# Weighted sums of an attention block moved from the scores' PSUM banks to the mix's banks, and inverse sums turned in row halves

## The chip, the cores and the metric

The kernel runs on one core of a Trainium2 chip. The metric is the device time of one execution in microseconds (us). Four compute engines work side by side, each through its own instructions in order: PE (matrix products, with its weight loads as a row of their own, PEld), DVE (vector), ACT (activations and copies) and POOL (elementwise work in SBUF). Transfers are issued from a fifth queue, SP. Results of PE land in PSUM, which has eight banks here, each of 512 fp32 values per partition.

## The reference, cut to what matters

```
# attention: q, k, v are (8 batches, 8 heads, 576, 64)
scores = q @ k.T / sqrt(64)
scores = where(scores >= 32nd largest of its row, scores, -1e9)
attn = exp(scores - max);  attn = attn / (sum(attn) + 1e-9)
x = (attn @ v), heads side by side          # (8, 576, 512)
# channel mix on x
x_prev = x moved down by one row
xk = mu_k*x + (1-mu_k)*x_prev;  xr = mu_r*x + (1-mu_r)*x_prev
k = max(xk @ w_k, 0);  v = k*k @ w_v        # 512 -> 1024 -> 512
r = sigmoid(xr @ w_r)
out = r * v
```

## The kernel before

The attention is cut into 288 tiles: one tile is 128 query rows against all 576 keys, as scores in 2 x 288 columns. Tiles form units of four (`U.w` = 4: two heads, two blocks of 128 rows), two or one; a unit shares one reciprocal of its row sums, one set of weighted sums and one write into `xT`, the transposed attention output. There are 112 units. A software pipeline runs over slots. In slot n it takes tile n in by `score` (PE) and `keep` (ACT copies the scores to SBUF), looks for candidates of tile n-1 (DVE), ranks tile n-2 (DVE), counts tile n-3 (ACT `count`, POOL `below`), exponentiates and masks tile n-4 (ACT `exp`, DVE `mask`), and turns tile n-5 (PE `turn_tile` and an ACT copy `et`). When the tile of n-6 is the last of its unit, the slot turns the unit's inverse sums (`inv`, which calls `turn_inverse`, followed by an ACT copy `ri`) and computes its weighted sums (`weigh`, PE); one slot later ACT copies these to SBUF (`sums`, which calls `take_sums`) and POOL multiplies them by the inverse sums (`place`).

Into the same slots the channel mix is fitted. It runs over 18 chunks of 256 rows of `xT`, each with 8 pieces of gates (`pz`), 16 of hidden values (`ph`) and 16 of output values (`pv`), 720 pieces in all. A piece is three PE products of 512 columns, or six of 256 columns. A gate group is 4 pieces, a hidden group 4, a value group 8. The products accumulate in a bank of the pool `psM`, which has two banks used in turn; a group's bank is emptied one slot after its last piece by ACT (`relu`, tanh) or DVE (`stt` at the step `first`). In the first 20 slots, before the mix can start, weight blocks are split into two parts through the same banks.

The order is set by hand: the table `ORDER` says in which order the steps of a slot are written, and so in which order they stand on each engine. How many pieces of the mix a slot gets is a planner's decision (`Lanes`, `work`): each slot adds 3.90 (`TENSOR`) to PE's budget, each step takes its own cost off (`L.use`), a piece costs 0.71, and pieces are written while the budget allows, at most 4 a slot. In the last 36 slots a piece costs 0.56. The planner's numbers are fixed in the code and are no measurements.

PSUM: the scores have two banks (`psS`, the tile `ps`), the exponentials two (`psE`), the turned tiles and the turned inverse sums two (`psT`), the mix two (`psM`). The weighted sums lie in columns 288 to 415 of the scores' banks:

```
g.ps = scored[:, :, :HS]                                        # HS = 288
g.sums = scored[:, :, HS:HS + 128], scored[:, 0, HS + 128:HS + 192]
```

Of the kernel before, what the change touches and what calls it, by code (L numbers as in the profile page):

```python
# [43 lines left out]
ORDER = """count below exp wpool high wmul norm evac best0 c0 drop0 c1 best1 c2 drop1 first score turn inv loads keep sums sign c3 best2 c4 bounds eighth norm2 et late act c5 early thr c6 mask place mix weigh wpe dve pool weights""".split()  # L44
# [3 lines left out]
def topk_attention_channel_mix(ctx: ExitStack, tc: tile.TileContext, q, k, v, mu_k, mu_r, w_k, w_v, w_r, out):  # L48
# [28 lines left out]
    def open_pools(stack, g, sfx):  # L77
# [17 lines left out]
        g.psM = p("psM", 2, space=PSUM)  # L95
# [24 lines left out]
    def weight_block(g, L, n, block, hi, lo, half):  # L120
# [8 lines left out]
        def remains(*more):  # L129
            W.lo = g.psM.tile([128, 512], F32, name="wlo", tag="pm")  # L130
            nc.tensor.matmul(W.lo, lhsT=ident, rhs=valf, start=True, stop=False)
            for i, x in enumerate(more):
                nc.tensor.matmul(W.lo, lhsT=x[0], rhs=x[1], start=False, stop=i == len(more) - 1)

        def fine():
            g.ready.append(nc.scalar.activation(lo, W.lo, AF.Copy, scale=scale))

# [17 lines left out]
        def shift():  # L155
            bits = g.psM.tile([128, 512], U32, name="wbits", tag="pm")
            nc.vector.tensor_scalar(bits, mag, 3, 0x3FFFFFFF, op0=OP.logical_shift_left, op1=OP.bitwise_and)
            nc.vector.scalar_tensor_tensor(val, high, 0xC0000000, bits, op0=OP.bitwise_and, op1=OP.bitwise_or)
            nc.vector.tensor_scalar(exp, val, 0xFF800000, None, op0=OP.bitwise_and)

# [141 lines left out]
    def turn_inverse(g, U, L):  # L302
        rb = U.rb.rearrange("p h d -> p (h d)")
        pr = g.pt[:, :, 384:]
        n = (U.w + 1) // 2
        for u in range(n):
            nc.tensor.transpose(pr[:, u], rb[:, u * 128:(u + 1) * 128], ident)  # L307

        def out_():
            U.ri = g.two.tile([128, 256], F32, name="ri")  # L310
            if U.w > 1:
                nc.scalar.activation(U.ri[:, :n * 128].rearrange("p (u q) -> p u q", u=n), pr[:, :n], AF.Copy)
            else:
                for j in range(2):
                    h = slice(j * 64, (j + 1) * 64)
                    nc.scalar.activation(U.ri[h, :64], pr[h, 0, h], AF.Copy)
# [18 lines left out]
    def take_sums(g, U):  # L335
# [4 lines left out]
        else:  # L340
            nc.scalar.activation(U.sum[:, :64], U.pa, AF.Copy)

# [49 lines left out]
    def hidden(g, f, part, xh, xl, hh, hl, n, X, L):  # L392
        if part == 0:
            X.ph = g.psM.tile([128, 2, CH], F32, name="ph", tag="pm")
# [8 lines left out]
        def relu():  # L403
            X.r = g.two.tile([128, 2, CH], F32, name="r")
            nc.scalar.activation(X.r[:, :, :n], ph[:, :, :n], AF.Relu)
        out_ = L.at(1, "evac", relu, "act", 0.46)
# [4 lines left out]
    def gate(g, t, m, h, xh, xl, G, L):  # L411
        if h == 0:
            G.pz = g.psM.tile([128, DM], F32, name="pz", tag="pm")
# [5 lines left out]
        def first():  # L419
            G.e = g.four.tile([128, DM], F32, name="eb")  # L420
            nc.scalar.activation(G.e[:m], pz[:m], AF.Tanh, scale=0.5)
        G.done = L.at(1, "evac", first, "act", 0.48)

    def value(g, t, m, hh, hl, f, G, row, L):
        if f == 0:
            G.pv = g.psM.tile([128, DM], F32, name="pv", tag="pm")
# [547 lines left out]
```

## Time and profile before

| | |
|---|---|
| median of 3 runs | 1203.48 us (1203.01 to 1204.04) |
| the profiled execution, its own time | 1202.92 us |
| span of its instructions | 1201.1 us |
| PE busy | 1115.5 us (93%) |
| DVE busy | 1078.9 us (90%) |
| POOL busy | 1025.5 us (85%) |
| ACT busy | 996.3 us (83%) |
| DMA | 78.79 MB, 24% of 16 engines' time |

Read it as three stretches: up to about 158 us the weights are prepared beside the first tiles; from 158 to 1117 us attention and mix run in the same slots; after the last score (1116.56 us) the pipeline empties and the last chunks of the mix remain. The span starts 1.8 us inside the execution's own time.

### The profile page before, as it was taken

How to read it: one execution, taken by the hardware profiler on the slowest of the kernel's cores; microseconds unless marked ns; L12 is line 12 of the kernel's file. 1: busy time of each engine (PE TensorE's matmuls, PEld its weight loads, DVE VectorE, ACT ScalarE, POOL GpSimd, SP SyncE). 2: the span in 40 equal slices, each digit the busy share in tenths (PEclk: the TensorE clock that was granted, in tenths of full speed). 3: DMA queues.
4: the chain of work that ended last, by engine and by line, in shares of the span. 5: the costliest groups of instructions: out<-in, count | busy, mean ns of one | idle time of the engine just before them, and what ended most of it. 6: DMA issues, size and time to landing. Idle time of an engine off the chain costs nothing.

```text
span 1201.1 us, 33093 instructions
## 1 busy us (share of the span) xinstructions
PE 1115.5 (93%) x10625; PEld 864.1 (72%) x10625; DVE 1078.9 (90%) x6287; ACT 996.3 (83%) x2121; POOL 1025.5 (85%) x1099
## 2 busy tenths in 40 slices
PE   4777899899999999999999999999999999999987
PEld 2443577676868787878787877787878777877876
DVE  4989999999999999999999999999999999999600
ACT  3777799898988899989898989998989899978621
POOL 5999987888889898989898888898989798988863
PEclk8788699899999999999999999999999999999998
DMA  5343124122322133212221124112321133111000
GB/s 171 99 135 98 30 49 107 47 54 60 87 71 55 49 89 76 58 47 58 67 58 47 43 77 101 50 43 67 100 73 44 48 86 87 46 39 39 29 10 29
DMA packets 161366, 78.79 MB, mean 66 GB/s; under 512 B 125344, under 2 KB 154016, under 8 KB 161184
## 3 DMA queue, kind: packets, MB, share of 16 engines
q1 hardware_dynamic: 161184, 76.59, 24.0%
q8 instruction: 87, 1.43, 0.5%
q14 instruction: 95, 0.78, 0.2%
HBM read 67.11 MB, written 9.44 MB: 64 GB/s over the span
## 4 chain that ended last, share of the span: by engine, by line
PE 50%; DVE 19%; ACT 14%; POOL 13%; issue 2%; SPq 1%; DMA 1%; DVEq 0%; ACTq 0%; POOLq 0%
PE ps L333 10%; PE ps L208 7%; DVE cand L241 4%; ACT sc L217 4%; PE pv L388 4%; DVE E L271 4%; PE ph L388 4%; PE pt L283 3%; PE pv L390 3%; PE pv L389 3%; DVE top L836 3%; POOL sg L260 3%; PE ph L389 3%; PE ph L390 3%; PE pz L388 2%; ACT sg L257 2%
## 5 line engine op out<-in xcount | busy, mean ns | idle before, releaser
L241 DVE MAX8 cand<-sc 128x8 f32<-128x82 f32 (+1 forms) x2016 | 468.0, 232 | 3.2 <-ACT sc L217 2.7
L260 POOL TENSOR_TENSOR sg<-sc,sg 128x576 f32<-128x576 f32 x288 | 410.9, 1428 | 38.3 <-ACT sg L257 36.7
L217 ACT ACTIVATE sc<-ps 128x576 f32<-128x576 f32 x288 | 187.9, 652 | 92.3 <-PE ps L208 80.6
L257 ACT ACTIVATE sg<-sc,seen 128x576 f32<-128x576 f32 x288 | 225.8, 784 | 26.0 <-DVE top L836 19.7
L271 DVE SCALAR_TENSOR_TENSOR E<-sc,seen,se 128x576 f32<-128x576 f32 x288 | 233.0, 809 | 0.4
L268 ACT ACTIVATE se<-sc,seen 128x576 f32<-128x576 f32 x288 | 215.8, 749 | 17.0 <-DVE E L271 16.2
L836 DVE MAX8 top<-sg 128x8 f32<-128x576 f32 x288 | 216.5, 752 | 3.3 <-POOL sg L260 2.9
L208 PE MATMUL ps<-K,qs 64*128 64x288 f32 x1024 | 202.4, 472 | 14.5 <-ACT sc L217 6.4
L286 ACT ACTIVATE et<-pt 128x640 f32<-128x640 f32 x288 | 204.6, 710 | 6.2 <-PE pt L307 3.0
L333 PE MATMUL ps<-et,v_in 128*64 128x128 f32 (+1 forms) x2560 | 165.3, 273 | 21.4 <-ACT sc L217 18.6
L283 PEld LDWEIGHTS pt<-ident,E 64*128 64x128 f32 x2880 | 134.0, 140 | 66.7 <-ACT sg L257 16.1
L244 DVE MAX8 top<-cand 128x8 f32<-128x56 f32 x864 | 177.4, 205 | 0.1
L388 PE MATMUL ph<-xh,wk 128*128 128x256 f32 x576 | 172.0, 299 | 0.0
L333 PEld LDWEIGHTS ps<-et,v_in 128*64 128x64 f32 x2560 | 134.5, 141 | 51.3 <-ACT sc L217 37.3
L389 PE MATMUL ph<-xl,wk 128*128 128x256 f32 x576 | 163.1, 283 | 0.0
L390 PE MATMUL ph<-xh,wk 128*128 128x256 f32 x576 | 162.8, 283 | 0.0
L283 PE MATMUL pt<-ident,E 64*128 64x64 f32 x2880 | 141.3, 226 | 5.7 <-DVE E L271 3.3
L208 PEld LDWEIGHTS ps<-K,qs 64*128 64x128 f32 x1024 | 80.6, 192 | 75.0 <-issue 29.6
L388 PE MATMUL pv<-wv,hh 128*128 128x512 f32 x288 | 122.0, 424 | 0.0
L390 PE MATMUL pv<-wv,hl 128*128 128x512 f32 x288 | 114.2, 397 | 7.2 <-POOL hl L409 7.2
L384 POOL TENSOR_TENSOR xl<-xm,xh 128x512 fp32r<-128x512 f32 x72 | 91.2, 1287 | 34.6 <-ACT xh L383 34.5
L247 DVE MATCH_REPLACE8 cand<-top,cand 128x56 f32<-128x56 f32 x576 | 115.6, 201 | 0.0
(92 smaller groups left out, 2359.0 us busy)
## 6 DMA issues: line engine op xcount, KB each, us to landing
v_in<-in_v SPq DMA_DIRECT2D x192, 128.0 KB, 2.5
qs<-in_q SPq DMA_DIRECT2D x96, 128.0 KB, 2.8
K<-in_k SPq DMA_DIRECT2D x64, 144.0 KB, 3.0
out<-eb SPq DMA_DIRECT2D x36, 256.0 KB, 2.2
vr_in<-in_v SPq DMA_DIRECT2D x96, 32.0 KB, 2.4
hh<-in_moe_w_v SPq DMA_DIRECT2D x6, 512.0 KB, 3.6
qs<-in_q SPq DMA_DIRECT2D x32, 96.0 KB, 2.6
hh<-in_moe_w_k SPq DMA_DIRECT2D x5, 512.0 KB, 3.4
```

What stands on the lines that cost most here:

```text
L208: nc.tensor.matmul(g.ps[:, e], lhsT=P.qs[h, T.j, x:x + 128], rhs=P.K[h, T.j], start=True, stop=True)
L217: nc.scalar.activation(T.sc.rearrange("p (e k) -> p e k", e=2), T.ps, AF.Copy)
L241: nc.vector.max(T.cand[:, 8 * i:8 * i + 8], T.sc[:, CUTS[i]:CUTS[i + 1]])
L257: nc.scalar.activation(T.side, T.sc, AF.Sign, bias=T.under, scale=-BELOW, accum_out=T.cnt)
L260: nc.gpsimd.tensor_mul(T.side, T.sc, T.side)
L271: nc.vector.scalar_tensor_tensor(T.e, T.sc, T.thr, g.pe, op0=OP.is_ge, op1=OP.mult, accum_out=T.rs)
L283: nc.tensor.transpose(g.pt[:, n, c * 64:(c + 1) * 64], T.e[h, k0:k0 + 128], ident[h, h])
L333: nc.tensor.matmul(pa[hs[j]], lhsT=lhsT, rhs=ms[c][j], start=(c == 0), stop=(c == NKC))
L388: nc.tensor.matmul(ps, lhsT=sh, rhs=mh, start=first, stop=False)
L389: nc.tensor.matmul(ps, lhsT=sh, rhs=ml, start=False, stop=False)
L390: nc.tensor.matmul(ps, lhsT=sl, rhs=mh, start=False, stop=last)
L836: nc.vector.max(M.top[:, 24:32], M.side)
```

## The change

Five things change. (1) `psM` becomes one buffer for each of two tags, handed out in turn by `bank`, and flags in the builder (`g.full`) record whether a bank's contents have been written out. (2) `weigh` asks `borrow` for a bank: if the one that comes next in turn is marked empty and all weight blocks are ready, the weighted sums go there (a tile named `pa`); otherwise they go to the scores' banks as before. Borrowing does not advance the turn. (3) In `ORDER`, `sums` stands ahead of `keep`. (4) `turn_inverse` turns 64-row halves, two for each former transpose, into the two banks of `pt`, as `turn_tile` does. (5) The planner's costs of a unit fall by 0.25 (0.1 for single ones) and of a turn by 0.1.

```diff
-ORDER = """... turn inv loads keep sums sign c3 ..."""
+ORDER = """... turn inv loads sums keep sign c3 ..."""
...
-        g.psM = p("psM", 2, space=PSUM)
+        psM = p("psM", 1, space=PSUM)
+        g.turn, g.full = 0, [False, False]
+        def bank(shape, name, dtype=F32):
+            i, g.turn = g.turn, 1 - g.turn
+            g.full[i] = True
+            return psM.tile(shape, dtype, name=name, tag=f"pm{i}"), i
+        def borrow(shape):
+            i = g.turn
+            if g.full[i] or len(g.ready) < 3 * HP + NFB:
+                return None
+            g.full[i] = True
+            return psM.tile(shape, F32, name="pa", tag=f"pm{i}"), i
+        def free(i):
+            g.full[i] = False
...
         for u in range(n):
-            nc.tensor.transpose(pr[:, u], rb[:, u * 128:(u + 1) * 128], ident)
+            for i, h in enumerate(hs):
+                nc.tensor.transpose(pr[:, i, hs[u]], rb[h, u * 128:(u + 1) * 128], ident[h, h])
...
         if u == 0:
-            U.pa = g.sums[U.w == 1]
+            U.pa, U.at = g.borrow([128, 2, 128] if U.w > 1 else [128, 64]) or (g.sums[U.w == 1], None)
...
+        if U.at is not None:
+            g.free(U.at)
...
-                    L.use("pe", 0.9 * ((W.U.w + 1) // 2) + 0.7 if W.U.w > 1 else 0.7)
+                    L.use("pe", 0.9 * ((W.U.w + 1) // 2) + 0.45 if W.U.w > 1 else 0.6)
...
-                    L.use("pe", 0.2)
+                    L.use("pe", 0.1)
```

`bank` and `free` also stand where the mix and the weights take and empty their banks. Line numbers after the change are larger by up to 28.

On PE, in a slot with the sums of a four-tile unit (the 87th after the first), before:

```order
L208 MATMUL ps<-K,qs 128x288 x2
L283 MATMUL pt<-ident,E 128x64 x10
L307 MATMUL pt<-ident,rb 128x128 x2
L333 MATMUL ps<-et_5828,v_in 64x128
L333 MATMUL ps<-et_5887,v_in 64x128
...
L333 MATMUL ps<-et_6041,vr_in_78 64x128
L208 MATMUL ps<-K,qs 128x288 x2
```

and in the same slot now:

```order
L229 MATMUL ps<-K,qs 128x288 x2
L304 MATMUL pt<-ident,E 128x64 x10
L330 MATMUL pt<-ident,rb 128x64 x4
L355 MATMUL pa<-et_5973,v_in 64x128
L355 MATMUL pa<-et_6041,v_in 64x128
...
L355 MATMUL pa<-et_6195,vr_in_78 64x128
L229 MATMUL ps<-K,qs 128x288 x2
```

The sums stand in the same place and write another bank; two turns of 128 columns became four of 64.

On ACT, in the slot that copies the sums of one unit in the main stretch, before (`sc` is written by `keep`, `sum` by `take_sums`, `r` by `relu`):

```order
L268 ACTIVATE se<-sc,seen 128x576
L405 ACTIVATE r<-ph 128x512
L217 ACTIVATE sc<-ps 128x576
L339 ACTIVATE sum<-ps 128x128
L286 ACTIVATE et_3701<-pt 128x2x5x64
```

and now:

```order
L289 ACTIVATE se<-sc,seen 128x576
L429 ACTIVATE r<-ph 128x512
L361 ACTIVATE sum<-pa 128x128
L238 ACTIVATE sc<-ps 128x576
L307 ACTIVATE et_3803<-pt 128x2x5x64
```

The copy of the sums moved ahead of the copy of the scores.

On POOL, from the last unit's write into `xT` on, before (`xd`, `xm`, `xl` belong to the last chunk's inputs; `r` and `hl` are hidden values, the first four such rows those of the chunk before it):

```order
L345 TENSOR_TENSOR xT<-sum,ri 128x256
L358 TENSOR_TENSOR xd_20645<-xT 128x512
L363 TENSOR_SCALAR xm<-xd_20645,nmu 128x256 x2
L368 TENSOR_TENSOR xm<-xm,xT 128x512
L408 TENSOR_TENSOR r<-r 128x512
L409 TENSOR_TENSOR hl<-r,hh 128x512
L384 TENSOR_TENSOR xl<-xm,xh 128x512 x2
L408 TENSOR_TENSOR r<-r 128x512
L409 TENSOR_TENSOR hl<-r,hh 128x512
L363 TENSOR_SCALAR xm<-xd_20468,nmu 128x256 x2
```

and now:

```order
L434 TENSOR_TENSOR hl<-r,hh 128x512
L369 TENSOR_TENSOR xT<-sum,ri 128x256
L382 TENSOR_TENSOR xd_20957<-xT 128x512
L387 TENSOR_SCALAR xm<-xd_20957,nmu 128x256 x2
L392 TENSOR_TENSOR xm<-xm,xT 128x512
L408 TENSOR_TENSOR xl<-xm,xh 128x512 x2
L387 TENSOR_SCALAR xm<-xd_20613,nmu 128x256 x2
```

The hidden values of the chunk before the last, two groups of which stood behind this write, all stand ahead of it now.

## Rows read from the trace of the kernel before

**Rows 1.** Main stretch: us, busy PE, PEld, DVE, ACT, POOL; PE's clock, DMA.
```profile
158.00:1117.00 959.00, 929.48 (x9440) 738.52 (x9442) 930.91 (x5576) 858.89 (x1859) 842.81 (x929) 1.00 0.25 64
```

**Rows 2.** Chain that ended last, 216 to 232 us: start, us, what.
```profile
218.60 0.82 DVE E L271 x2
...
229.15 0.82 DVE E L271 x2
```

**Rows 3.** Who waited for whom, 158 to 1117 us: total us, times, longest.
```profile
PE ps L333 <- ACT sc L217: 13.9, 19, 1.3
...
DVE rs L295 <- ACT rs L291: 9.3, 20, 0.9
...
ACT sc L217 <- PE ps L208: 69.4, 104, 2.9
```

**Rows 4.** PE in order of time, one slot with sums: start, us, idle before.
```profile
375.82 0.28 PE L389 MATMUL ph<-xl,wk 128*128 128x256 f32 x1
375.94 0.28 PE L390 MATMUL ph<-xh,wk 128*128 128x256 f32 x1
376.15 0.76 PE L208 MATMUL ps<-K,qs 64*128 64x288 f32 x4
376.74 0.47 PE L283 MATMUL pt<-ident,E 64*128 64x64 f32 x10
377.14 0.44 PE L307 MATMUL pt<-ident,rb 128*128 128x128 f32 x2
378.01 1.09 PE L333 MATMUL ps<-et,v_in 128*64 128x128 f32 x16 [0.44 <-ACT sc L217]
...
380.35 0.76 PE L208 MATMUL ps<-K,qs 64*128 64x288 f32 x4
...
381.34 0.39 PE L388 MATMUL ph<-xh,wk 128*128 128x256 f32 x1
```

**Rows 5.** ACT in order of time, the same place.
```profile
377.31 0.66 ACT L217 ACTIVATE sc<-ps 128x576 f32<-128x576 f32 x1
...
381.15 0.65 ACT L217 ACTIVATE sc<-ps 128x576 f32<-128x576 f32 x1 [0.41 <-PE ps L208]
381.70 0.38 ACT L339 ACTIVATE sum<-ps 128x256 f32<-128x256 f32 x1
```

**Rows 6.** PE in order of time: a single turn of inverse sums.
```profile
240.35 0.33 PE L307 MATMUL pt<-ident,rb 128*128 128x128 f32 x1
240.44 0.36 PE L388 MATMUL ph<-xh,wk 128*128 128x256 f32 x1
```

**Rows 7.** PE in order of time: the last score, the last sums, the last chunk.
```profile
1116.24 0.39 PE L390 MATMUL pz<-wr,xl 128*128 128x512 f32 x1
1116.56 0.76 PE L208 MATMUL ps<-K,qs 64*128 64x288 f32 x4
...
1143.37 0.39 PE L333 MATMUL ps<-et,vr_in 128*64 128x128 f32 x4
...
1156.82 0.40 PE L388 MATMUL pz<-wr,xh 128*128 128x512 f32 x1
...
1157.81 0.63 PE L388 MATMUL pz<-wr,xh 128*128 128x512 f32 x1
...
1163.91 0.39 PE L388 MATMUL pv<-wv,hh 128*128 128x512 f32 x1
...
1169.51 0.28 PE L388 MATMUL ph<-xh,wk 128*128 128x256 f32 x1
```

**Rows 8.** POOL in order of time, after the last weighted sums.
```profile
1144.27 0.74 POOL L345 TENSOR_TENSOR xT<-sum,ri 128x256 f32<-128x256 f32 x1 [1.31 <-ACT sum L339]
...
1147.25 1.30 POOL L368 TENSOR_TENSOR xm<-xm,xT 128x512 f32<-128x512 f32 x1
...
1150.88 2.52 POOL L384 TENSOR_TENSOR xl<-xm,xh 128x512 fp32r<-128x512 f32 x2
...
1165.30 2.54 POOL L384 TENSOR_TENSOR xl<-xm,xh 128x512 fp32r<-128x512 f32 x2 [5.20 <-ACT xh L383]
```

More of the change, by code (lines that the diff above doesn't have):

```diff
@@ L43 @@
 EXPS, EVAC = 4, (0, 'et')
-ORDER = """count below exp wpool high wmul norm evac best0 c0 drop0 c1 best1 c2 drop1 first score turn inv loads keep sums sign c3 best2 c4 bounds eighth norm2 et late act c5 early thr c6 mask place mix weigh wpe dve pool weights""".split()
+ORDER = """count below exp wpool high wmul norm evac best0 c0 drop0 c1 best1 c2 drop1 first score turn inv loads sums keep sign c3 best2 c4 bounds eighth norm2 et late act c5 early thr c6 mask place mix weigh wpe dve pool weights""".split()
 @with_exitstack
@@ L94, in open_pools @@
         g.psT = p("psT", 1, space=PSUM)
-        g.psM = p("psM", 2, space=PSUM)
+        psM = p("psM", 1, space=PSUM)
[12 more added lines that the diff above has]
+            g.full[i] = False
+        g.bank, g.borrow, g.free = bank, borrow, free
     def load_mu():
@@ L129, in remains @@
         def remains(*more):
-            W.lo = g.psM.tile([128, 512], F32, name="wlo", tag="pm")
+            W.lo, W.at = g.bank([128, 512], "wlo")
             nc.tensor.matmul(W.lo, lhsT=ident, rhs=valf, start=True, stop=False)
@@ L136, in fine @@
             g.ready.append(nc.scalar.activation(lo, W.lo, AF.Copy, scale=scale))
+            g.free(W.at)
         L.at(2, "wpool", coarse)
@@ L155, in shift @@
         def shift():
-            bits = g.psM.tile([128, 512], U32, name="wbits", tag="pm")
+            bits, at = g.bank([128, 512], "wbits", U32)
             nc.vector.tensor_scalar(bits, mag, 3, 0x3FFFFFFF, op0=OP.logical_shift_left, op1=OP.bitwise_and)
@@ L159, in shift @@
             nc.vector.tensor_scalar(exp, val, 0xFF800000, None, op0=OP.bitwise_and)
+            g.free(at)
         L.at(1, "sign", magnitude)
@@ L393, in hidden @@
         if part == 0:
-            X.ph = g.psM.tile([128, 2, CH], F32, name="ph", tag="pm")
+            X.ph, X.at = g.bank([128, 2, CH], "ph")
         ph, e, half = X.ph, part // 2, part % 2
@@ L405, in relu @@
             nc.scalar.activation(X.r[:, :, :n], ph[:, :, :n], AF.Relu)
+            g.free(X.at)
         out_ = L.at(1, "evac", relu, "act", 0.46)
@@ L412, in gate @@
         if h == 0:
-            G.pz = g.psM.tile([128, DM], F32, name="pz", tag="pm")
+            G.pz, G.at = g.bank([128, DM], "pz")
         pz = G.pz
@@ L421, in first @@
             nc.scalar.activation(G.e[:m], pz[:m], AF.Tanh, scale=0.5)
+            g.free(G.at)
         G.done = L.at(1, "evac", first, "act", 0.48)
@@ L425, in value, with gated @@
         if f == 0:
-            G.pv = g.psM.tile([128, DM], F32, name="pv", tag="pm")
+            G.pv, G.to = g.bank([128, DM], "pv")
         three(G.pv[:m], hh[:, f, t:t + m], hl[:, f, t:t + m], wv[0][:, f, :], wv[1][:, f, :], f == 0, f == NFB - 1)
         if f == NFB - 1:
-            L.at(1, "first", lambda: nc.vector.scalar_tensor_tensor(G.e[:m], G.e[:m], 1.0, G.pv[:m], op0=OP.add, op1=OP.mult),
-                 "dve", 0.6)
+            def gated():
+                nc.vector.scalar_tensor_tensor(G.e[:m], G.e[:m], 1.0, G.pv[:m], op0=OP.add, op1=OP.mult)
+                g.free(G.to)
+            L.at(1, "first", gated, "dve", 0.6)
             G.out = L.at(2, "dma", lambda: nc.sync.dma_start(row, G.e[:m]))
```

8 lines of the change are left out of this document (4 added, 4 removed).

## The prediction, made before the change was run

> **What bounds the kernel now.** I read the busy times by stretch first, then the chain of waits, then the tables of who waits for whom, then the order of time in single slots and at the end.
>
> In the main stretch PE is busy 929.5 of 959.0 us and DVE 930.9 [rows 1]: two engines within 3% of full, neither with much room. DVE's floor is seen where the chain runs on DVE alone: four masks stand in 218.60 to 229.15 us, so a slot takes 10.55 / 3 = 3.52 us [rows 2]. DVE is not waiting there, and no edit here makes it faster. PE, by contrast, is what ACT waits for: the copy of the scores waited 69.4 us in 104 places for the score [rows 3]. So PE is late against ACT, DVE is nearly full, and what the change can free in the main stretch is bounded by DVE's idle time, 959.0 - 930.9 = 28 us. After the last score the limits are others: a chain of PE, ACT and POOL work with gaps.
>
> **The change part by part.**
>
> *The wait ahead of the weighted sums.* In a slot with sums PE does score, turn, inverse turn, and then stands: at 378.01 the sums had waited 0.44 us for the copy of the scores [rows 4], which ran from 377.31 to 377.97 [rows 5]. The two touch different columns of the same bank. In the main stretch this waiting sums to 13.9 us [rows 3]. By the order, 91 of the 106 slots with sums between the weight blocks and the last score now borrow; 15 still go behind the scores. I take 13.9 x 91 / 106 = 12 us of PE time back.
>
> *The inverse turns.* A single one takes 240.44 - 240.35 = 0.09 us [rows 6]. Ten transposes of 64 columns take 377.14 - 376.74 = 0.40 us, of which a step like that between the hidden products and the score, (376.15 - 375.94) - (375.94 - 375.82) = 0.09, is the change to another shape [rows 4]; so a pair of halves costs 0.31 / 5 = 0.06. 148 turns between the weights and the last score save 0.03 each, 4.4 us. Where sums follow the turn directly, one change of shape falls away too: by the order 25 such slots remain, 2.2 us. Together 6 to 7. The Trainium skill (TensorEngine Tiling (Array Packing), section Key Properties) says that a change of tiling mode drains the engine. By that rule alone the fewer changes of shape would be the gain; the rows agree that a change costs something, about 0.09 us.
>
> *The copy of the sums ahead of that of the scores.* At 381.15 ACT had stood 0.41 us waiting for a score, and only at 381.70 did it take the sums [rows 5], whose products stand ahead of the score of 380.35 [rows 4]. The 0.38 us copy now fits into that wait. What it delays, where ACT is late, is the copy of the scores: 0.26 us or so to the next start, at most 112 times, behind which stand the copy of the turned tile and the next count. I price it at nothing; the cover is the 69.4 us that ACT waits there [rows 3]. Without that cover it costs up to 0.38 x 112 = 43 us of ACT, with 100 us of ACT idle in the main stretch [rows 1].
>
> *A new wait.* A mix group that opens the borrowed bank waits for the copy of the sums. By the order 63 slots after a borrow open a group, and in 27 that group's first product is the first thing after score and turn. In [rows 4] that place is 381.34; a copy begun at the latest at 381.15 would be over at 381.53, so such a group would wait 0 to 0.2 us: 0 to 5 us in all, and I take 1. Queued behind the opening product on PE are that slot's other pieces and the next score.
>
> *The planner.* Its costs fall by about 34 us over the run (80 units by 0.25, 32 by 0.1, 112 turns by 0.1), more than the 12 + 6.5 that PE really gets. So it writes pieces earlier. By the order, 123 products of 512 columns follow the last score where 162 did (192 of 256 columns both times). 39 products at (1169.51 - 1163.91) / 24 = 0.233 us [rows 7], 9.1 us of PE, move from the end into the main stretch. There PE's need changes by -12 - 6.5 + 1 + 9.1 = -8.4 us. But they are bunched more: of the 261 slots between the weights and the last score, those with no piece and no sums rise from 4 to 12, while those with four pieces stay (79 and 80 in all). A slot of four hidden pieces needs 0.59 + 0.40 + 24 x 0.12 + 0.09 = 3.96 us of PE [rows 4], 0.44 over DVE's 3.52, and an empty one about 1.1, 2.4 under it. Eight more empty slots could idle PE for up to 19 us. The bounds for the main stretch are therefore -8.4 - 3 (the latter if DVE's own waits on ACT, 9.3 us at the reciprocal [rows 3], shrink by a third) and -8.4 + 19 = +10.6; I take -3, since a PE that is late fills part of an empty slot with what it has behind it, and since the largest term, the 12 us, is spread over the whole stretch.
>
> *The end.* Before, the last sums end near 1143.76 and the last chunk's gates start at 1156.82 [rows 7], 13.1 us later. In between POOL writes `xT` at 1144.27, finishes the chunk's input by 1148.55, spends 2.3 us on a group of hidden values, and starts `xl` only at 1150.88 [rows 8]; PE stands behind a value product that needs the next such group. In the new order no hidden group of the chunk before is left there. The chain is then 0.5 us to the write, 4.3 to 1148.55, and half of `xl`, 1.26: the gates can start about 6.1 us after the sums, 7.0 earlier, with 18 value products (4.2 us) ahead of them as cover. Next, 24 value products used to stand between gates and hidden products, 1163.91 to 1169.51; now the hidden products follow the gates directly and wait for `xl`, which ended at 1167.84 [rows 8], so 1.7 us less. Against this, PE has more to do between the last score and the last sums: 33 products of 512 columns and 96 of 256 where there were 42 and 66, (33 - 42) x 0.233 + 30 x 0.12 = +1.5 us, less 0.2 for the turns. After an idle of 3 us the gates ran at spacings of 0.43 (1157.81 is one of eight rows of 0.63) instead of 0.23, 1.6 us lost [rows 7]; the new order has two such gaps, of about 2 and 2.5 us, so it loses 0 to 3.2, that is 1.6 less to 1.6 more than before. The Trainium skill (TensorE: Matmul & The Clock Gate, section HAM oscillation) says that idle gaps put the clock back to its lower level; the rows agree for the one gap there. Sum: -7.0 - 1.7 + 1.3 = -7.4, bounds -9.0 and -5.8, wider by 1 each way since the chain is put together from single rows. I take -8, since the shorter gap probably keeps the clock.
>
> *The start.* Up to 158 us weight blocks set the pace and the sums go behind the scores as before. At the seam a wait of about 1 us of the same kind goes: -0.5.
>
> **Sum.** 1202.92 (the profiled execution; its span, 1201.1, and 1.8 around it) - 3 - 8 - 0.5 = 1191.4. The median of the runs is 0.6 above that execution, so 1192.
>
> **Rivals.**
> (a) *The main stretch gives all that PE frees.* ACT waits for PE so often that 8.4 us of PE come through, and DVE's idle time of 28 us has room for it: 1203.5 - 11.4 - 9 = 1183. For it: the 69.4 us. Against it: the empty slots.
> (b) *The end's gain is eaten by the bunches.* Main stretch +6, end -7: 1202. A PE that starts the long slots 0.4 us late each pushes scores, counts and the eighth maximum behind DVE's floor. For it: 80 slots of four pieces. Against it: the same number before.
> (c) *Slower: groups wait for the copy of the sums.* If ACT, no longer waiting for PE, comes to the sums late, the 27 groups right behind a turn pay. From a mean of 0.45 us (27 x 0.45 = 12) the gain is gone; at 0.6 us with the main stretch's bunching at +4 it is 1203.5 - 8.5 + 4 + 16 - 8 = 1207. Against it: now ACT stands waiting in 104 slots.
> (d) *The clock.* With more gaps on PE the granted clock, 1.00 (2.4 GHz) through the main stretch [rows 1] in spite of 29.5 us of idle time there, could fall: twelve empty slots each followed by 1.6 us lost are 19 us: 1211. The Trainium skill (TensorE: Matmul & The Clock Gate, section on psum-queue depth-cycling) describes just that for a kernel that cycles PSUM banks. In this trace the gaps of up to 1.3 us [rows 3] did not bring it.
> (e) *It doesn't do what it says*: the banks are seldom empty. Excluded by the order, 91 of 106; only the time is open.
>
> **How the numbers follow.** Forecast 0.62 (its own range 1187 to 1198), (a) 0.20 (1180 to 1187), (b) 0.11 (1198 to 1204), (c) 0.04, (d) 0.03. A run of this kernel can tell 0.2%, 2.4 us, from no change. Faster: forecast, (a), and half of (b), 0.87; same: the other half of (b) and a little of (c), 0.07; slower 0.06. The range 1183 to 1201 leaves out some of (a), the upper end of (b), (c) and (d), 2 in 10.
>
> **What would show it.** Right: the wait of the sums for the scores' copy falls from 13.9 us to under 3; ACT's wait for scores shrinks; the gates of the last chunk start 6 to 7 us after the last sums; the last score stands within 5 us of 1116. Wrong: products of the mix that wait for `sum`; DVE's idle time over 28 us; a granted clock under 1.00 in the main stretch; or a last score before 1108, which would be (a).

## The result

The change makes the kernel slower. Four runs of the changed kernel have a median of 1220.97 us (1218.36 to 1221.35), beside 1203.76 us (1203.01 to 1204.79) for the kernel before: a ratio of 1.0141, with a 95% interval of 1.0128 to 1.0154, or 17 us where a gain of 11 had been forecast. The profiled execution took 1218.36 us.

In the changed kernel, line 229 is the score (208 before), 304 the turn (283), 330 the inverse turn (307), 355 the weighted sums (333), 238 the copy of the scores (217), 361 and 363 the copies of the sums (339, 341), 412 to 414 the mix (388 to 390), 434 the hidden values `hl` (409).

First the busy times of the main stretch, with the columns of [rows 1]; it now ends at 1143, since the last score starts at 1142.47 us instead of 1116.56:

```profile
158.00:1143.00 985.00, 944.17 (x9622) 750.42 (x9624) 934.53 (x5581) 860.06 (x1863) 847.76 (x935) 0.98 0.24 62
```

The stretch is 26 us longer. PE is busy 14.7 us more and idle 985.0 - 944.2 = 40.8 us, 11.3 more than in [rows 1]; DVE does what it did (+3.6) and its idle time grows from 28 to 50 us. PE's granted clock has a mean of 0.98 instead of 1.00. Then the waits of PE in that stretch, as in [rows 3] (total us, times, longest):

```profile
PE pv L414 <- POOL hl L434: 15.0, 17, 2.4
PE ps L229 <- ACT sc L238: 11.7, 11, 1.4
PE pt L304 <- DVE top L265: 4.0, 11, 1.1
PE ph L412 <- ACT sum L361: 3.9, 8, 1.5
PE pt L330 <- POOL rb L321: 2.8, 3, 1.4
PE ph L412 <- ACT sum L363: 1.6, 2, 1.2
```

The wait that headed the list before, the sums for the scores' copy (13.9 us), is gone. In its place stand value products that wait for POOL's hidden values (3.9 us before), scores that wait until ACT has copied the score before them out of their two banks (1.9 us before), and groups that wait for the sums (none before). Waits of other engines in the same stretch:

```profile
ACT sc L238 <- PE ps L229: 64.8, 101, 4.5
```

```profile
DVE rs L316 <- ACT rs L312: 19.6, 27, 1.4
DVE cand L262 <- ACT sc L238: 12.8, 22, 2.1
```

and, for the second of DVE's waits, before:

```profile
DVE cand L241 <- ACT sc L217: 1.3, 5, 0.4
```

ACT's wait for scores changed little (69.4 before), so PE is still late against it. DVE's wait at the reciprocal has doubled (9.3 before), and its wait for the copied scores is ten times what it was. By these two DVE stands 10.3 + 11.5 = 21.8 us longer, nearly all of the 22 us by which its idle time grew. DVE is the other engine with little room, so the longer stretch is read there too: it does the same work and waits for copies that come late. And the end, PE in order of time, as in [rows 7]:

```profile
1142.47 0.76 PE L229 MATMUL ps<-K,qs 64*128 64x288 f32 x4
...
1143.46 0.50 PE L412 MATMUL pv<-wv,hh 128*128 128x512 f32 x1
1143.80 0.39 PE L413 MATMUL pv<-wv,hh 128*128 128x512 f32 x1
...
1171.17 0.39 PE L355 MATMUL ps<-et,vr_in 128*64 128x128 f32 x4
...
1175.80 0.40 PE L412 MATMUL pz<-wr,xh 128*128 128x512 f32 x1
...
1177.61 0.50 PE L414 MATMUL pz<-wr,xl 128*128 128x512 f32 x1 [1.19 <-POOL xl L408]
...
1184.09 0.38 PE L412 MATMUL ph<-xh,wk 128*128 128x256 f32 x1 [1.20 <-ACT xh L407]
...
1208.40 0.39 PE L414 MATMUL pv<-wv,hl 128*128 128x512 f32 x1
```

The last sums end at 1171.17 + 0.39 = 1171.56. The last chunk's gates start 4.2 us after that (13.1 before); the first product of them that reads POOL's `xl` starts 1177.61 - 1171.56 = 6.05 us after the sums. The last value product ends 66.3 us after the last score (75.8 before). So the end gave 9.5 us, and the main stretch took 26.

What a bunched stretch looks like, PE in order of time:

```profile
699.13 0.76 PE L229 MATMUL ps<-K,qs 64*128 64x288 f32 x4
699.72 0.47 PE L304 MATMUL pt<-ident,E 64*128 64x64 f32 x10
701.61 0.76 PE L229 MATMUL ps<-K,qs 64*128 64x288 f32 x4 [1.42 <-ACT sc L238]
702.57 0.58 PE L304 MATMUL pt<-ident,E 64*128 64x64 f32 x10 [0.20 <-DVE top L265]
702.90 0.46 PE L330 MATMUL pt<-ident,rb 64*128 64x64 f32 x4
703.29 0.79 PE L412 MATMUL pv<-wv,hh 128*128 128x512 f32 x1
703.88 0.63 PE L413 MATMUL pv<-wv,hh 128*128 128x512 f32 x1
705.22 0.79 PE L414 MATMUL pv<-wv,hl 128*128 128x512 f32 x1 [0.71 <-POOL hl L434]
705.94 1.34 PE L355 MATMUL pa<-et,v_in 128*64 128x128 f32 x10
```

POOL in order of time, the same place:

```profile
702.77 1.05 POOL L433 TENSOR_TENSOR r<-r 128x512 f32<-128x512 f32 x1
703.89 1.27 POOL L434 TENSOR_TENSOR hl<-r,hh 128x512 fp32r<-128x512 f32 x1
```

The granted clock around it (columns as in [rows 1]):

```profile
697.00:704.00 7.00, 5.38 (x43) 3.65 (x43) 5.58 (x39) 7.00 (x16) 5.60 (x7) 0.92 0.05 12
704.00:711.00 7.00, 6.29 (x57) 5.03 (x55) 5.57 (x29) 2.89 (x8) 4.21 (x4) 0.59 0.00 1
```

The slot of 699.13 holds a score and a turn and nothing else. PE is through after about 1 us and stands 1.42 us until ACT, which is busy for all of 697 to 704 us, has copied that score, so that the next one can use its banks. The value piece that follows needs `hl`, which POOL finishes at 703.89 + 1.27 = 705.16: PE goes on at 705.22. From 704 to 711 us the granted clock is 0.59, largely the lower of the two levels (1.2 GHz for 2.4). It had fallen before the wait of 0.71 us: the first two products of the piece already start 0.59 us apart, where the same step behind a turn takes 1143.80 - 1143.46 = 0.34 us at the end of this trace.

### The profile page after: what moved, and what is told of

Read it like the earlier page. It is cut to its first block, busy times and chain, and to the rows that moved or that the text cites. A ratio compares the mean times of both kernels' runs of the same rounds, so it can differ in the third digit from the quotient of the medians.

```text
span 1216.6 us, 33388 instructions
## 1 busy us (share of the span) xinstructions
PE 1119.6 (92%) x10785; PEld 867.3 (71%) x10785; DVE 1081.8 (89%) x6287; ACT 995.6 (82%) x2121; POOL 1023.7 (84%) x1099
## 4 chain that ended last, share of the span: by engine, by line
PE 59%; POOL 17%; DVE 10%; ACT 10%; issue 2%; SPq 1%; DMA 0%; DVEq 0%; ACTq 0%; POOLq 0%
PE ps L229 9%; PE pa L355 8%; PE ph L412 6%; PE ph L413 4%; PE ph L414 4%; PE pv L412 4%; PE pt L304 4%; PE pv L414 4%; POOL sg L281 4%; PE pv L413 4%; PE pz L412 3%; POOL xl L408 3%; PE pz L414 2%; PE pz L413 2%; POOL hl L434 2%; ACT sc L238 2%
## 5 line engine op out<-in xcount | busy, mean ns | idle before, releaser
L262 DVE MAX8 cand<-sc 128x8 f32<-128x82 f32 (+1 forms) x2016 | 464.7, 231 | 14.8 <-ACT sc L238 14.6
L304 PEld LDWEIGHTS pt<-ident,E 64*128 64x128 f32 x2880 | 134.1, 141 | 69.9 <-ACT sg L278 11.7
L355 PE MATMUL pa<-et,v_in 128*64 128x128 f32 (+1 forms) x2128 | 142.5, 279 | 0.0
L355 PEld LDWEIGHTS pa<-et,v_in 128*64 128x64 f32 x2128 | 116.4, 143 | 20.4 <-issue 9.8
L414 PE MATMUL pv<-wv,hl 128*128 128x512 f32 x288 | 116.7, 405 | 15.0 <-POOL hl L434 15.0
L412 PEld LDWEIGHTS ph<-xh,wk 128*128 128x128 f32 x576 | 109.9, 191 | 15.8 <-ACT sum L361 6.2
```

The source lines that it names most:

```text
L262: nc.vector.max(T.cand[:, 8 * i:8 * i + 8], T.sc[:, CUTS[i]:CUTS[i + 1]])
L304: nc.tensor.transpose(g.pt[:, n, c * 64:(c + 1) * 64], T.e[h, k0:k0 + 128], ident[h, h])
L355: nc.tensor.matmul(pa[hs[j]], lhsT=lhsT, rhs=ms[c][j], start=(c == 0), stop=(c == NKC))
L412: nc.tensor.matmul(ps, lhsT=sh, rhs=mh, start=first, stop=False)
L414: nc.tensor.matmul(ps, lhsT=sl, rhs=mh, start=False, stop=last)
```

## The experiments

Theories as the expectations name them. A: the planner's lower costs change the plan, by bunching pieces into slots of four with empty ones between them (A1), by moving work from the end into the main stretch (A2), or by setting pieces into slots that have sums (A3). B: the new order on ACT delays the copy of the scores. C: mix groups wait for the copy of the sums out of a borrowed bank.

All runs, with the ratio to runs of the kernel before that were taken beside them (medians of 1203.4 to 1204.6 us; where the text gives a difference to the kernel before in us, it is to 1203.8). The plan's columns are counted in the order of the program, over 261 slots between the weights and the last score: slots of four pieces without sums, and slots with neither pieces nor sums. "Low" is PE's time at the lower clock between 158 us and the last score, in us, summed over short stretches as 2 x (1 - granted clock) x their length where the clock is under 0.99. "hl" is PE's wait for hidden values there.

| run | us | ratio (95%) | four | empty | hl | low |
|---|---|---|---|---|---|---|
| before | 1203.8 | 1 | 78 | 4 | 3.9 | 6.8 |
| after | 1220.97 | 1.0141 (1.0128 to 1.0154) | 77 | 12 | 15.0 | 30.5 |
| e1_old_costs | 1194.21 | 0.9924 (0.9907 to 0.9940) | 78 | 4 | 7.8 | 13.6 |
| e2_costs_only | 1224.95 | 1.0178 (1.0161 to 1.0195) | 77 | 12 | 14.0 | 20.4 |
| e3_keep_first | 1235.82 | 1.0271 (1.0254 to 1.0288) | 77 | 12 | 14.5 | 17.0 |
| e4_no_borrow | 1225.55 | 1.0186 (1.0169 to 1.0203) | 77 | 12 | 13.5 | 17.0 |
| e5_new_costs_less_pace | 1202.05 | 0.9982 (0.9971 to 0.9992) | 65 | 6 | 14.4 | 10.2 |
| e6_old_costs_more_pace | 1202.43 | 0.9985 (0.9973 to 0.9996) | 97 | 12 | 6.6 | 13.6 |
| e7_three_pieces | 1192.60 | 0.9908 (0.9892 to 0.9925) | 0 | 5 | 4.4 | 6.8 |
| e8_old_costs_keep_first | 1205.94 | 1.0016 (1.0006 to 1.0026) | 78 | 4 | 6.7 | 13.6 |
| e9_three_then_four | 1191.05 | 0.9895 (0.9879 to 0.9912) | 13 | 5 | 6.5 | 6.8 |
| e10_halves_only | 1206.33 | 1.0018 (1.0008 to 1.0028) | 78 | 4 | 4.0 | 6.8 |
| e11_costs_three_pieces | 1193.05 | 0.9905 (0.9887 to 0.9922) | 0 | 5 | 5.7 | 6.8 |
| e12_fill | 1262.87 | 1.0487 (1.0469 to 1.0504) | 77 | 12 | 8.8 | 54.5 |
| e13_fill_mix_bank | 1214.16 | 1.0081 (1.0064 to 1.0098) | 77 | 12 | 15.7 | 13.6 |
| e14_balanced | 1198.57 | 0.9955 (0.9939 to 0.9972) | 50 | 4 | 12.7 | 6.8 |
| e15_unbalanced | 1235.79 | 1.0265 (1.0248 to 1.0283) | 78 | 12 | 19.9 | 37.4 |
| e16_values_later | 1205.23 | 1.0014 (1.0004 to 1.0023) | 74 | 11 | 0 | 17.0 |
| e17_three_values_later | 1202.82 | 0.9984 (0.9971 to 0.9996) | 15 | 8 | 0 | 13.6 |
| e18_balanced_later | 1199.08 | 0.9950 (0.9934 to 0.9967) | 54 | 7 | 0 | 6.8 |

### Which part of the change

**e1_old_costs**: the kernel after with the planner's costs of before. The pieces then stand slot for slot as in the kernel before; banks, order and halves are new.

```diff
-L.use("pe", 0.9 * ((W.U.w + 1) // 2) + 0.45 if W.U.w > 1 else 0.6)
+L.use("pe", 0.9 * ((W.U.w + 1) // 2) + 0.7 if W.U.w > 1 else 0.7)
...
-L.use("pe", 0.1)
+L.use("pe", 0.2)
```

> The changed kernel with the planner's old costs: every piece of the mix stands in the slot in which it stood before, and only the banks, the copy of the sums ahead of the scores' copy and the half turns remain of the change. Theory A (the lower costs bunch the mix, and PE then idles, falls to the lower clock and comes late to the scores): the 13.9 us of waits go and nothing is bunched, so 1187 to 1197. Theory B (the copy of the sums ahead of the scores' copy makes ACT stand for the sums and delays the scores' copy): still slower than before, 1210 or more. Theory C (mix groups wait for the copy of the sums in the borrowed bank): about 1205, with waits of the mix for the sums of over 10 us.

**e2_costs_only**: the kernel before with only the planner's new costs (the same two lines the other way round); the pieces stand as in the kernel after.

> The kernel before with the planner's new costs alone: pieces stand in the slots of the changed kernel, banks, order and turns are the old ones. Theory A: slower than before, by as much as the changed kernel or more, since the waits of the sums remain: 1218 to 1235. Theories B and C: the end gains 9 us and the main stretch stays, so 1190 to 1200.

Measured: 1194.21 and 1224.95 us. The main stretch of the first and of the second, columns as in [rows 1]:

```profile
158.00:1107.00 949.00, 922.77 (x9562) 736.42 (x9559) 928.48 (x5572) 860.31 (x1858) 841.34 (x928) 0.99 0.25 64
```

```profile
158.00:1148.00 990.00, 947.38 (x9489) 750.87 (x9489) 937.29 (x5588) 861.76 (x1865) 850.77 (x935) 0.99 0.24 62
```

Two lines of the planner, which compute nothing, are worth 1220.97 - 1194.21 = 26.8 us with the new banks and 1224.95 - 1203.8 = 21.2 us without them. The rest of the change gains: 9.6 us on the old plan, 4.0 on the new one.

**e10_halves_only**: the kernel before with only the inverse turns in halves.

```diff
-    nc.tensor.transpose(pr[:, u], rb[:, u * 128:(u + 1) * 128], ident)
+    for i, h in enumerate(hs):
+        nc.tensor.transpose(pr[:, i, hs[u]], rb[h, u * 128:(u + 1) * 128], ident[h, h])
...
```

> The kernel before with the turns of the inverse sums by row halves alone; pieces, banks, order as before. By the sum of the prediction 4.4 us of turns and 2 to 4 of changes of shape are saved on the tensor engine: 1196 to 1199. If the vector engine hides them: 1202 to 1204.

Measured: 1206.33 us, 2.5 us slower rather than faster, outside both expectations. The stretch from 158 to 1120 us (the last score starts at 1119.96), and PE's first wait in it:

```profile
158.00:1120.00 962.00, 922.35 (x9609) 737.10 (x9604) 932.91 (x5593) 859.95 (x1864) 844.11 (x930) 1.00 0.25 63
```

```profile
PE ps L334 <- ACT sc L217: 25.4, 42, 1.6
```

PE is busy 7.1 us less than in [rows 1] and idle 10.1 us more. The sums waited for the scores' copy 13.9 us in 19 places [rows 3] and now wait 25.4 in 42. What the shorter turn saves ahead of a wait goes into the wait; why the stretch is 3 us longer beyond that isn't shown.

**e4_no_borrow**: the kernel after, but no bank is ever borrowed.

```diff
-            if g.full[i] or len(g.ready) < 3 * HP + NFB:
+            if True:
```

> The changed kernel that never borrows: all sums go behind the scores, pieces stand as in the changed kernel. Theory A: the waits of the sums come back on top, 1220 to 1235. Theory C: 6 us faster than the changed kernel, about 1214. Theory B: about as the changed kernel.

Measured: 1225.55 us. On the new plan the banks are worth 4.6 us, and their new waits do not make the change slow (against C as the main cause). Without them the early copy and the halves gain nothing there: e2, which has neither, took 1224.95 us.

**e3_keep_first** and **e8_old_costs_keep_first**: the kernel after, and e1, each with the copy of the scores ahead of that of the sums again.

```diff
-... inv loads sums keep sign ...
+... inv loads keep sums sign ...
```

> The changed kernel with the copy of the scores ahead of that of the sums again. Theory A: like the changed kernel, 1217 to 1225. Theory B: 1190 to 1205, and the vector engine's wait for the scores' copy falls from 13 us to under 4. Theory C: a few us slower than the changed kernel, since the borrowed bank comes free later.

> Run e1 (old costs, borrowed banks, half turns) with the copy of the scores ahead of that of the sums again; pieces stand as before. If the copy of the sums is what groups that open the borrowed bank wait for (theory C, seen in run e3 as 23 us of such waits against 6 in the changed kernel), 5 to 15 slower than e1, 1199 to 1209. If the order on the activation engine matters only where the mix is bunched, like e1, 1192 to 1196.

Measured: 1235.82 and 1205.94 us, 14.9 and 11.7 slower than with the new order; so B is wrong (DVE's wait for the copied scores, which was to fall from 13 us to under 4, is 14.0 us in e3). The direction is C's, but e3 lost more than any of the theories had. PE's waits for the sums on the old plan, 158 to 1121.5 us:

```profile
PE ph L412 <- ACT sum L361: 9.6, 11, 2.4
...
PE ph L412 <- ACT sum L363: 3.0, 4, 1.1
```

They were 4.5 and 1.1 us in e1. Borrowing needs the early copy: without it the groups wait, and the gain of the banks is gone. Whether the halves add anything beside the borrowed banks was not run.

### Which property of the plan

**e5_new_costs_less_pace**: the kernel after with PE's budget of a slot at 3.82 instead of 3.90. **e6_old_costs_more_pace**: e1 with 4.02.

> The changed kernel with 3.82 instead of 3.90 of budget a slot: as many pieces before the last score as in the changed kernel (646), 143 of them in slots with sums (146 there), but 65 slots of four pieces instead of 77 and 6 empty ones instead of 12. Theory A1 (bunching: full slots that exceed the vector engine's slot, then empty ones): most of the loss goes, 1190 to 1205. Theory A2 (the 12 pieces moved into the main stretch cost it): like the changed kernel, 1216 to 1224. Theory A3 (pieces in the slots with sums are what costs): also 1216 to 1224.

> The old costs (run e1) with 4.02 instead of 3.90 of budget a slot, about as much budget in all as the new costs give: 634 pieces before the last score as before, 114 in slots with sums (105 before), but 97 slots of four pieces instead of 78 and 12 empty ones instead of 4. Theory A1: slower than e1 by 15 to 30, 1209 to 1225. Theories A2 and A3: like e1, 1190 to 1198.

Measured: 1202.05 and 1202.43 us. A budget smaller by 0.08 a slot gives back 18.9 us. It holds the same 123 products of 512 columns behind the last score and 143 pieces in slots with sums (146 after), so neither A2 nor A3 explains it, and A1 remains: 65 slots of four and 6 empty ones for 77 and 12. Its main stretch:

```profile
158.00:1124.00 966.00, 936.27 (x9656) 745.20 (x9657) 935.32 (x5603) 863.02 (x1868) 849.64 (x937) 0.99 0.25 63
```

PE is idle 11.1 us less than after the change and busy 7.9 us less, with the time at the lower clock down by 20.3 us; the wait for hidden values stays (14.4 us). The other way the loss was 8.2 us, under the 15 to 30 expected, although e6 has as many empty slots as the kernel after and more of four. So these two counts don't give the size of the loss; that it depends on where full and empty slots stand is likely, and not shown.

**e7_three_pieces**: the kernel after with at most three pieces in a slot. **e11_costs_three_pieces**: e2, that is without the banks, the order and the halves, with the same limit.

```diff
-PACE, TENSOR, SHARE, PIECE, CAP, MOST = 4.60, 3.90, 0.74, 0.71, 4.45, 4
+PACE, TENSOR, SHARE, PIECE, CAP, MOST = 4.60, 3.90, 0.74, 0.71, 4.45, 3
```

> The changed kernel with at most three pieces a slot: no slot of four, 5 empty ones, 184 pieces in slots with sums, and 632 pieces before the last score, so the end is as long as before. Theory A1: the last score comes at 1100 to 1107 us as in e1 or earlier, 1185 to 1196 in all. Theory A2: 1190 to 1197. Theory A3: slower than the changed kernel, over 1225.

> Run e2 (the kernel before with the new costs alone) with at most three pieces a slot: pieces stand as in run e7, sums behind the scores. Theory A1 (bunching): the loss of e2 goes, and what remains against e7 are the waits of the sums and the turns: 1198 to 1210. If the cap only helps together with the borrowed banks: 1218 to 1226.

Measured: 1192.60 and 1193.05 us, the same by their intervals. PE in the main stretch of the first:

```profile
158.00:1103.50 945.50, 926.12 (x9600) 736.28 (x9601) 930.00 (x5586) 863.14 (x1863) 841.30 (x927) 1.00 0.25 64
```

Idle are 19.4 us of PE, the clock is as in the kernel before (6.8 us at the lower level), and the lower costs stand. One limit takes back 28 us. And beside it the borrowed banks are worth nothing that can be measured, so e11 came out under the 1198 to 1210 expected: in e11 a piece stands between turn and sums in 40 of 41 slots with the sums of a four-tile unit, and the sums' wait for the scores' copy is 5.0 us there without any borrowing, where it was 13.9. In both runs DVE has 16 us of idle time left in the stretch, so no change on PE can gain much more there.

**e9_three_then_four**: e7, but four pieces are allowed in the last 24 slots.

```diff
-                work(MOST)
+                work(MOST if n < total - 24 else 4)
```

> The changed kernel with at most three pieces a slot up to the last 24 slots and four from there: 13 slots of four pieces, 5 empty ones, 642 pieces before the last score (632 in run e7, 646 in the changed kernel). If the bunching alone took back the gain, main stretch as in e7 and an end 7 us shorter: 1183 to 1189. If pieces moved ahead of the last score cost as much there as they save behind it: 1190 to 1196, as e7.

Measured: 1191.05 us, the lowest median of all, 1% under the kernel before; its interval overlaps those of e7 and e11. It holds 135 products of 512 columns behind the last score where e7 holds 165. Those 30 are 30 x 0.233 = 7 us of PE work moved ahead of it, and the run is 1.6 us shorter: the second expectation holds, by which moved pieces cost in the main stretch about what they save behind it.

**e14_balanced** and **e15_unbalanced**: the kernel after with a unit's cost at +0.2 (e15), which sets more pieces into slots with sums, and with the budget at 3.70 besides (e14).

```diff
-PACE, TENSOR, SHARE, PIECE, CAP, MOST = 4.60, 3.90, 0.74, 0.71, 4.45, 4
+PACE, TENSOR, SHARE, PIECE, CAP, MOST = 4.60, 3.70, 0.74, 0.71, 4.45, 4
...
-L.use("pe", 0.9 * ((W.U.w + 1) // 2) + 0.45 if W.U.w > 1 else 0.6)
+L.use("pe", 0.9 * ((W.U.w + 1) // 2) + 0.2 if W.U.w > 1 else 0.6)
```

> The changed kernel with 3.70 of budget a slot and a unit's cost lower by another 0.25: 642 pieces before the last score, 146 in slots with sums, 50 slots of four pieces, 4 empty ones. By what the tensor engine needs in any four slots in a row over what the vector engine needs there (19 us in sum; 17 in runs e1 and e7, 22 in e9, 25 in e5, 31 in the changed kernel), the last score at 1105 to 1112 us and 1184 to 1191 in all. If the number of four-piece slots were what counts: between e9 (13 of them) and e5 (65), 1194 to 1200. If pieces in slots with sums were: 1215 or more.

> The changed kernel with 3.90 of budget a slot and a unit's cost lower by another 0.25: again 642 pieces before the last score, 153 in slots with sums, 78 slots of four pieces, 12 empty ones; the same measure of bunching is 35 us. By it the last score at 1145 to 1158 us and 1223 to 1237 in all. If the moved work were what counts (642 pieces as in e9 and e14): 1188 to 1196.

Measured: 1198.57 and 1235.79 us. The direction is that of A1, and the two lie 37 us apart by the budget alone. The size of e14 was missed: it is 8 to 15 us over what PE's need above DVE's pace in runs of four slots gave (19 us for e14, 22 for the faster e9). That measure is not enough.

### What the bunching costs by

**e12_fill** and **e13_fill_mix_bank**: the kernel after with products that nobody reads in slots that hold neither pieces nor sums. In e12 they are 12 into spare columns of the turn's banks, in e13 five into the mix bank that is taken next, if it is empty. The edit of e13:

```diff
-                work(MOST)
+                if not work(MOST) and V and not last and 23 < n < total:
+                    got = g.borrow([128, 64])
+                    if got:
+                        for _ in range(5):
+                            nc.tensor.matmul(got[0], lhsT=ident, rhs=ident[:, :64], start=True, stop=True)
+                        g.free(got[1])
```

> The changed kernel with twelve idle products of 64 columns (identity by identity, read by nobody) in each of 13 slots that have neither pieces nor sums, about 1.3 us of work where the tensor engine would idle. If the lower clock after such gaps is a cause of its own: less time at the lower clock in the main stretch (about 30 us in the changed kernel) and 1208 to 1216. If it only goes with the bunching: 1218 to 1225.

> The changed kernel with five idle products of 64 columns, written to the next mix bank where it is empty, in each of the 13 slots without pieces and sums: about 0.6 us of work (at most 1.3) that waits for no other engine, unlike the products of run e12, which stood 2 us for a copy and then took 3 to 5 us. If the lower clock after gaps is a cause of its own: less than 15 us at the lower clock and 1208 to 1217. If the gaps and the clock only follow from the bunching: 1219 to 1228.

Measured: 1262.87 us, outside both expectations, and 1214.16. The first tells nothing on the clock, since its products add a wait of their own; PE in order of time:

```profile
516.18 5.21 PE L858 MATMUL pt<-ident 128*128 128x64 f32 x24 [2.02 <-ACT et L307]
```

They wait 2 us for the copy out of the turn's bank and then hold PE for 5.2 more. The second is the one to read. Its main stretch, and the added products alone in it (busy PE, PEld; clock, DMA):

```profile
158.00:1138.00 980.00, 951.02 (x9747) 758.71 (x9745) 935.14 (x5584) 860.49 (x1864) 848.14 (x935) 0.99 0.25 62
```

```profile
158.00:1138.00 980.00, 14.61 (x110) 13.10 (x110) 0.99 0.25 62
```

PE is busy 6.9 us longer than after, and the run is 6.8 us shorter. The added products take 14.6 us, more than the 11.8 us by which PE's idle time falls (40.8 to 29.0; the scores' wait for their copy goes from 11.7 to 0.8), so filling the gaps can't be the gain. All other work of PE takes 7.8 us less. The time at the lower clock falls from 30.5 to 13.6 us, half of which, 8.5 us, would give about that; the wait for hidden values stays (15.7). So the lower clock, not only the idle time itself, is a cause of its own.

**e16_values_later**, **e17_three_values_later**, **e18_balanced_later**: the kernel after, e9 and e14, each with one rule more: value products may stand two slots after the last write of their hidden values, not one.

```diff
-while not L.past(c.written[f // 2]) or ...
+while not (L.past(c.written[f // 2]) and getattr(c.written[f // 2], 'slot', -9) + 1 < L.slot) or ...
```

> The kernel after, with one rule more for the planner: a group of value products may begin only two slots after the last write of its hidden values, not one. PE's wait of 15.0 us for POOL's hidden values (17 waits of up to 2.4 us after the change) should nearly go. The lists of slots otherwise stay bunched: 74 slots of four pieces (77), 11 empty ones (12), and 159 products of 512 columns behind the last score where there were 123, so 36 x 0.233 = 8.4 us of PE work go from the main stretch to the end. Theory H, the late hidden values are a cause of their own: their wait falls under 4 us, the last score comes 8.4 + 8 to 11 us earlier, near 1124 to 1126, the end grows by about 8, and the run takes 1209 to 1214. Theory N, they are only where a bunched PE happens to stand: another wait takes their place (the scores' copy, the sums), the last score comes only 6 to 9 us earlier and the run takes 1218 to 1223.

> The balanced kernel (PE's budget 3.70, a unit's cost +0.2; 1198.57 us, where 1184 to 1191 had been expected) with the rule of the run before: value products two slots after the last write of their hidden values. It waits 12.7 us for POOL's hidden values in the main stretch without the rule. The plan has 54 slots of four pieces (50), 7 empty ones (4), and 180 products of 512 columns behind the last score where there were 142, so 38 x 0.233 = 8.9 us of PE work go to the end. Theory H: the wait was what the measure of bunching had left out; the main stretch falls by 8.9 + 8 to 12 us, the end grows by 8.9, and the run takes 1186 to 1192. Theory N: the wait's place is taken by others and the run stays within 1196 to 1200.

> The fastest kernel so far (three pieces a slot until the last 24 slots; 1191.05 us) with the same rule. It waits 6.5 us for POOL's hidden values in the main stretch without it. Behind the last score stand 192 products of 512 columns (135) and 210 of 256 (192), so 57 x 0.233 + 18 x 0.12 = 15.4 us of PE work go to the end. Theory H: that wait goes too, the main stretch falls by 15.4 + 3 to 6 us, but part of the end is not full of PE work, so it grows by 10 to 15: 1182 to 1191. Theory N: with so few bunched slots the wait costs nothing, the main stretch falls by no more than 12 because DVE is its limit, and the run takes 1192 to 1197.

Measured: 1205.23 (e16), 1199.08 (e18) and 1202.82 us (e17). The main stretch and PE's first waits in e16, 158 to 1120 us:

```profile
158.00:1120.00 962.00, 930.94 (x9615) 742.17 (x9613) 934.56 (x5593) 864.95 (x1864) 843.60 (x931) 0.99 0.25 63
```

```profile
PE ps L229 <- ACT sc L238: 10.1, 14, 1.4
PE pt L330 <- POOL rb L321: 9.0, 9, 1.4
PE pt L304 <- DVE top L265: 4.9, 11, 1.2
```

On the bunched plan the run is 15.7 us shorter by the medians without the wait for hidden values (11.5 between the two profiled executions), at least what theory H gave (1209 to 1214). The main stretch loses 23 us, of which PE's busy time 13.2 (8.4 for products moved to the end, and the lower clock falls to 17.0 us) and PE's idle time 9.8; the rest of the 15.0 us came back as waits for `rb`. The end grows by 10.9. So the wait is a cause too, for at most 9.8 us; 5 to 7 us more of the gain are the clock's, and the plan itself is a little less bunched (74 and 11 for 77 and 12). On the other two plans the wait goes and nothing is gained (theory N, or worse): there the main stretch becomes shorter by 10.5 us in e18, just the products moved (its expectation counted 142 behind the last score in e14, the trace has 135, so 45 x 0.233 = 10.5 us), and by 1.4 in e17, for 15.4 moved, and the end takes more than that back, since the rule also holds up the last chunk: its gates start 18.2 and 23.4 us after the last sums, where they start 7.0 in e9. So e14's miss is not explained by this wait and stays open.

## Why the prediction was wrong

**The step that failed is that on the planner.** It named the twelve empty slots and their bound ("could idle PE for up to 19 us"), and then took -3 for the main stretch, "since a PE that is late fills part of an empty slot with what it has behind it". Measured: +26, beyond its upper bound of +10.6. On the kernel's other parts alone (e1) the same stretch gave 959 - 949 = 10 us of gain, so the lower costs took 36 us of it and gave some 9.5 back at the end. What the sum had wrong about them:

- *Idle time.* An empty slot is not filled by work that PE is late with. The rows at 699 us show why: the next score needs the banks that ACT has not emptied, so PE stands although work is queued behind that score. The bound itself counted idle time in the eight new empty slots alone, and neither the waits that bunched pieces bring elsewhere nor the clock. It isn't the count of empty slots that sets the loss: e6 has 12 of them too and lost 8 us. PE's idle time rose by 11.3 us where the waits of the sums had given back 13.9.
- *Hidden values.* Bunched pieces bring value products up to POOL's `hl`, 15.0 us where it had been 3.9. The prediction looked at this wait in the end alone, and no rival had it. In e16, without it, PE is idle 9.8 us less in the main stretch. It seems the smaller part of the loss: e5 keeps 14.4 us of it and still takes back 18.9 of the 26.8 us between the changed kernel and e1.
- *The clock*, rival (d), had 0.03 because gaps of up to 1.3 us had not brought it down. That misread the trace of before: the mean of 1.00 in [rows 1] hides a fall to the lower level, right behind a wait of 1.57 us. PE in order of time, and the stretch from there (columns as in [rows 1]):

```profile
232.22 1.33 PE L208 MATMUL ps<-K,qs 64*128 64x288 f32 x4 [1.57 <-ACT sum L341]
```

```profile
232.20:239.00 6.80, 6.70 (x43) 5.56 (x45) 6.80 (x45) 5.79 (x13) 6.15 (x9) 0.50 0.00 0
```

After the change the clock stood at the lower level for 30.5 us instead of 6.8, which costs about (30.5 - 6.8) / 2 = 12 us of PE. That is under (d)'s 19, and e13 gives 7 us of it back with products that do nothing. The Trainium skill (TensorE: Matmul & The Clock Gate, section "A second HAM failure mode: psum-queue depth-cycling") says that frequent short idle spells between groups of products can make the clock swing between its levels; the trace agrees, with waits of at most 2.4 us on PE. The rule was the better guide here, and was given too small a chance.
- *Moved work*, 9.1 us by the prediction's own sum, is in the +26 too, and the end gives it back.

By busy time that makes, from before to after: +9.1 moved, +12 clock, -7.1 turns and shapes (922.35 in e10, whose time at the lower clock is that of before, for 929.48 in [rows 1]; 6 to 7 had been forecast) = +14, measured +14.7. With +11.3 idle time that is the +26. The terms are good to some 3 us: in e1 PE is busy 922.77 us although it has 6.8 us more at the lower clock. How much of the idle time each kind of bunching owns can't be split further: the waits stand in for each other, as `rb` did in e16.

**What was right.** The wait of the sums for the scores' copy is gone, and e1, whose end is as long as before, gains 9.6 us, all of it in the main stretch, where the terms freed 12 + 6.5 on PE. The copy of the sums ahead of that of the scores costs nothing that shows, and is needed (e3, e8). The groups' new wait, priced at 1 within 0 to 5, was 3.9 + 1.6 in the waits shown and about 6 with the smaller ones, a little over its bound: rival (c) in kind, at half its price or less. The end gave 9.5 where 8 had been taken, within its bounds with the 1 us added. The chain over POOL was priced right: the first gate product that needs `xl` starts 6.05 us after the sums, for 6.1. The gates themselves start at 4.2 us, as soon as the 18 value products ahead of them are done, since their first two products read only ACT's `xh`. And the clock stayed up through these shorter gaps, as had been taken: the rows behind 1177.61 follow at 0.23 us.

**The halves** were priced as 6 to 7 us of PE. PE is busy that much less, but alone they gain nothing (e10): their time lies ahead of a wait, and the prediction should have said so, as its own row of 378.01 in [rows 4] shows that wait right behind the turn.

**Its own signs.** The text named as signs of being wrong a DVE idle for over 28 us, a clock under 1.00 and products that wait for `sum`. All three came. Of its signs of being right the fall of the sums' wait came; the last score, to stand within 5 us of 1116, stood 26 us after it.

## What to carry to other kernels

When a change frees time on an engine that a planner feeds, correcting the planner's costs is a second change: run it apart, since here it turned 9.6 us of gain into 17 of loss. An average within the budget says little; look at how heavy and empty slots follow each other, since an empty slot is only slack if the next step needs nothing from others. And before pricing a shorter step, look at what stands right behind it: time saved ahead of a wait goes into the wait, and a wait that any other work could cover (one piece between turn and sums, e11) needs no new bank.

## What the runs showed of the hardware

The granted clock fell with PE busy for most of the time around: two 7 us stretches in a row with 5.38 and 6.29 us busy had 0.92 and 0.59 in the changed kernel, after waits of 1.42 and 0.20 us, and in the kernel before it stood at 0.50 from 232.2 us on, right behind a wait of 1.57 us. Five small products in each of 13 empty slots were enough to take 17 us of such time away, and to pay for themselves.

A product in another shape than the one ahead of it cost about 0.09 us more on PE, by the prediction's reading of [rows 4]; with the inverse turns in the shape of the turn ahead of them PE was busy 7.1 us less in e10, where that reading gave 6 to 7.
